# A second landing buffer for float64 weight blocks, and their transfers put forward in the queue, in an attention and mixture-of-experts kernel

## The chip, the cores and the metric

The kernel runs on one core of a Trainium2 chip. The metric is the time of one execution on the device in microseconds (us). Three runs of the kernel before took 558.76, 559.46 and 561.17 us; their median, 559.46 us, is the time to compare with. A separate profiled execution took 557.68 us.

## What is computed

Attention over 8 batches of 8 heads, 576 positions, head size 64, with a block-causal mask of blocks of 64; its output, 4608 rows of 512, goes through a soft mixture of 8 experts, and that through a gated product:

```python
scores = scale * q @ k.T                      # per batch and head, masked, softmax, @ v
logits = x @ phi                              # x: 4608 x 512, phi: 512 x 32
slot_input = softmax(logits, over rows).T @ x
slot_out[e] = relu(slot_input[e] @ w1[e]) @ w2[e]        # 8 experts, 4 slots each
x = softmax(logits, over slots) @ slot_out
a, b = x @ moe2_w1, x @ moe2_w2
out = (a * b) @ moe2_w3 @ moe2_w_out
```

The four matrices named moe2 arrive as float64 (their draws are divided by a float64 number); the kernel narrows them to float32 itself.

## The kernel before

**Attention.** It is tiled by pairs of heads: 32 pairs, numbered n, four to a batch b. For a pair, SP loads queries and keys (`ld`, line 493) and values (`ldv`, 497). ACT and POOL split queries and keys in a high and a low part (506, 513). TensorE makes score tiles for the row maxima (`M`, 526), DVE reduces them (`R`, 530), TensorE turns the maxima (`mT`, 552), ACT copies them out (564), and four small transfers on SP spread them over a row (`mx`, 573 to 575). TensorE then makes the scores (`Q`, 584), ACT the exponentials (`E`, 607), POOL three sums of exponential tiles for the denominators (`P0`, `P1`, `P3`, 617), TensorE the products with the values (`V`, 632 and 636) and the denominators (`SU`, 648, which needs POOL's three sums), and DVE adds these up (664, 666).

**Once per batch, beside the pairs of the next one.** DVE takes reciprocals of the denominators (672), SP writes them to DRAM (`rw`, 677 and 678) and reads them back, each row repeated on 64 partitions (`rd1`, `rd2`, `rd0`, `rd3`, two reads each, 683). POOL multiplies the attention output by them (`sx`, 688, four instructions of which two come ahead of a sum of the pair at hand and two behind it). Then follow the logits (697), transposes (754) and the slots' inputs (803, 805) on TensorE.

**The blocks.** Beside the attention, 28 blocks of 128 rows by 512 float64 numbers (128x1024 in 32-bit words) are narrowed, numbered j: 0 to 7 of w_out, 8, 9, 26 and 27 of w3, 10 to 17 of w1 (into the tile wA), 18 to 25 of w2 (into wB, whose four rows of 1024 fill in order; blocks 24 and 25 write row 3). A block is loaded by one transfer on SP (`bl`, line 1022) into the first 1024 columns of the tile vt; ACT squares the high words (`bm`, 1035), DVE puts the bits together in three instructions (`b1`, `b2`, `b3`: 1028, 1030, 1032) and a fourth writes the narrowed block (`b4`, 1037). All blocks share the one buffer in vt, so the transfer of block j waits for the readers of block j-1.

**What sets the order.** `Plan` holds every step as an operation with an engine, a duration, what it waits for and a due time. `Plan.order` simulates the engines and gives one list, sorted by the simulated start; each engine executes its part of that list strictly in order. SP issues all transfers, so a transfer that waits holds up those behind it. The line that names the waits of a block's transfer is

```python
op("bl", "SP", .43, old(j - 1, "b3", "bm") or [("Q0", 2)], lat=3.5, due="b", ...)
```

**After the attention** (from about 317 us) come the last batch's logits, the product of w3 and w_out (1130), the experts (1151 to 1172, whose weights stream in 2 MB transfers, 1054), and from about 420 us the products 1292, 1355 and 1357 that make the output.

Of the kernel before, what the change touches and what calls it, by code (L numbers as in the profile page):

```python
# [11 lines left out]
I32 = mybir.dt.int32  # L12
# [19 lines left out]
def warm(nc, keep, ps, n, w=128):  # L32

    for _ in range(n):
# [8 lines left out]
           Q0=(36.7116, -4.3567, 26.3714, 15.8153), Q1=(52.1613, 19.992, 71.6173, 44.2372),  # L43
# [39 lines left out]
WAIT = dict(PE=0.0, DVE=10616.85007, ACT=6722.41331, POOL=7334.5673, SP=12439.66901)  # L83
PERIOD, HELD, SLIP, WIN0, WIN1 = 100.0, 8, 0.1, 20, 29
BG0, BGS = 3.0, 1.0
BESIDE = {8: 0, 9: 2, 26: 4, 27: 6}
LATE_W3 = [i for i in range(16) if i not in BESIDE.values()]
PLACE = (0, 4, 1, 5, 2, 6, 3, 7)
# [11 lines left out]
class Plan:  # L100
# [213 lines left out]
    def op(self, key, eng, dur, after=(), banks=0, free=None, mode="full", lat=None, due=None, late=0., load=0., filler=False):  # L314
# [2 lines left out]
                             free=free if free is None or isinstance(free, tuple) else (free, key[1]),  # L317
                             mode=mode if eng == "PE" else None, due=self.due(key[0] if due is None else due) + late)

    def order(self):  # L320
        ops, INF = self.ops, 1e18
        free = dict(PE=4., DVE=2., ACT=2., POOL=3.5, SP=.7)
        bank, held, done, mode, out, queue = [0.] * BANKS, {}, {}, None, [], 0.
        waits, then, ready = {k: len(o["after"]) for k, o in ops.items()}, {}, {e: {} for e in free}
        row = deque(sorted((k for k in ops if ops[k]["eng"] == "PE" and not ops[k]["filler"]), key=lambda k: (ops[k]["due"], ops[k]["at"])))
        fill = deque(k for k in ops if ops[k]["filler"])
        for k, o in ops.items():
            for a in o["after"]:
                then.setdefault(a, []).append(k)
            if not waits[k]:  # L330
                ready[o["eng"]][k] = 0.
        pairs = lambda: [max(bank[i:i + 2]) for i in range(0, BANKS, 2)]
        space = lambda n: min(pairs()) if n == 2 else min(bank) if n else 0.
        while len(out) < len(ops):
            best = None
            for e, R in ready.items():
                can = []
                for k in R if e != "PE" else [k for k in (*list(row)[:1], *list(fill)[:1]) if k in R]:
                    o = ops[k]
                    turn = TURN[mode][o["mode"]] if e == "PE" and mode is not None and o["mode"] != mode else 0.  # L340
                    t = max(R[k], free[e] + turn, space(o["banks"]))
                    if t < INF:
                        can.append((t, k))
                if e == "PE" and len(can) == 2:
                    can = can[1:] if can[1][0] + ops[can[1][1]]["dur"] <= can[0][0] + SLIP else can[:1]
                if can:
                    first = min(t for t, _ in can)
                    c = min((x for x in can if x[0] <= first + LOOK[e]), key=lambda x: (ops[x[1]]["due"] + WAIT[e] * (x[0] - first), ops[x[1]]["at"]))
                    if best is None or c[0] < best[0]:
                        best = c[0], e, c[1]  # L350
            t, e, k = best
            o, slot, idle = ops[k], None, t - free[e]
            del ready[e][k]
            end = t + o["dur"]
            if e == "PE":
                (fill if o["filler"] else row).popleft()
                turn = TURN[mode][o["mode"]] if mode is not None and o["mode"] != mode else None
                if t > free[e] + .01 and not (turn is not None and t <= free[e] + turn + 1e-9):
                    end += ENTRY[o["mode"]]
                mode = o["mode"]  # L360
            if o["banks"] == 2:
                p = pairs()
                i = 2 * p.index(min(p))
                slot = held[k] = (i, i + 1)
            elif o["banks"]:
                can = [i for i in range(BANKS) if bank[i] <= t + 1e-9]
                slot = held[k] = (max(can, key=lambda i: (bank[i ^ 1], -i)) if can else bank.index(min(bank)),)
            for i in slot or ():
                bank[i] = INF
            free[e] = end  # L370
            done[k] = end + o["lat"]
            if e == "SP":
                queue = max(queue, end + 1.3) + o["load"]
                done[k] = max(done[k], queue + .7)
            if o["free"]:
                for i in held[o["free"]]:
                    bank[i] = done[k]
            out.append((t, len(out), k, slot, idle if e == "PE" and k[1] < 2 else 0.))
            for a in then.get(k, ()):
                waits[a] -= 1  # L380
                if not waits[a]:
                    ready[ops[a]["eng"]][a] = max(done[x] for x in ops[a]["after"])
        return [o[2:] for o in sorted(out)]
# [14 lines left out]
class Attn:  # L398
# [577 lines left out]
        self.constants()  # L976

    def run(self):
        for (name, n), slot, idle in Plan(self.nb).order():
            if idle > .5 and (name[0] in "MQ" or name == "mT") and n < 2:  # L980
                warm(self.nc, self.keep, self.bank(slot), int(4.5 * idle - 1), 256)
            f = getattr(self, "op_" + name, None) or getattr(self.rest, "op_" + name, None)
            if f:
                f(n, slot)
            else:
                f = getattr(self, "op_" + name[:-1], None) or getattr(self.rest, "op_" + name[:-1])
                f(n, slot, int(name[-1]) if name[-1].isdigit() else name[-1])


class Rest:  # L990
# [3 lines left out]
    def __init__(self, tc, ctx, io, keep):  # L994
        self.tc, self.nc, self.io, self.keep, self.ctx = tc, tc.nc, io, keep, ctx
        self.pre_ctx = ctx.enter_context(ExitStack())
        self.pre = self.pre_ctx.enter_context(tc.tile_pool(name="pre", bufs=1))
        self.right = ctx.enter_context(tc.tile_pool(name="right", bufs=1, side="right"))
        self.vt = self.pre.tile([128, 1280], F32, name="vt")
        self.wA, self.wB = (self.pre.tile([128, 4, 1024], F32, tag=f"w{m}", name=f"w{m}") for m in "AB")  # L1000
        self.wO = self.pre.tile([128, 8, 512], F32, name="wO")
        self.w01 = self.pre.tile([128, 2, 512], F32, tag="w01", name="w01")
        self.wo_t, self.w3_t = {}, {}
        self.w2 = self.right.tile([128, 512], F32, name="w2")
        self.win, self.u64, self.f64, self.W, self.pairs, self.wos, self.w_terms = {}, {}, {}, {}, {}, {}, {}
        self.st, self.hT, self.stages = {}, {}, {}

    def background(self, j, step, slot):

        nc = self.nc  # L1010
        if j < 8:
            src, dst = self.io["w_out"][128 * j:128 * j + 128], self.wO[:, j]
        elif j in BESIDE:
            i = BESIDE[j]
            src, dst = self.io["w3T"][i // 2, i % 2], self.f(i)
        else:
            w, src = ((self.wA, "moe2_w1"), (self.wB, "moe2_w2"))[(j - 10) // 8]
            row, f = (j - 10) % 8 // 2, 512 * (j % 2)
            src, dst = self.io[src][128 * row:128 * row + 128, 2 * f:2 * f + 1024], w[:, row, f:f + 512]
        if step == "l":  # L1020
            self.raw64 = self.vt[:, 0:1024].bitcast(I32)
            nc.sync.dma_start(out=self.raw64, in_=src)
            return
        v = self.raw64.rearrange("p (n t) -> p n t", t=2)
        lo, hi = v[:, :, 0], v[:, :, 1]
        if step == 1:
            u = self.ub = self.attn.bank(slot).bitcast(I32)
            nc.vector.tensor_scalar(u, hi, 3, 0x3fffffff, op0=ALU.logical_shift_left, op1=ALU.bitwise_and)
        elif step == 2:
            nc.vector.scalar_tensor_tensor(self.ub, hi, -0x40000000, self.ub, op0=ALU.bitwise_and, op1=ALU.bitwise_or)  # L1030
        elif step == 3:
            nc.vector.scalar_tensor_tensor(self.ub, lo, 29, self.ub, op0=ALU.logical_shift_right, op1=ALU.bitwise_or)
        elif step == "m":
            self.m64 = self.vt[:, 1024:1280].bitcast(mybir.dt.bfloat16)
            nc.scalar.activation(out=self.m64, in_=hi.bitcast(F32), func=AF.Square)
        else:
            nc.vector.scalar_tensor_tensor(dst, self.m64, 1.024e-9, self.ub.bitcast(F32), op0=ALU.is_ge, op1=ALU.mult)
# [505 lines left out]
```

## Time and profile before

| what | value |
|---|---|
| median of three runs | 559.46 us |
| profiled execution: whole / span of the instructions | 557.68 / 555.8 us |
| TensorE busy | 543.1 us, 98% |
| DVE, POOL, ACT busy | 394.3, 334.0, 322.6 us |
| granted TensorE clock | 1.000 |
| moved by DMA | 116.97 MB, mean 210 GB/s |

The span is the time from the first instruction to the last; 1.9 us of the execution lie around it. A busy TensorE is not one at its peak, because ends of matmuls are modelled; where it waits is better read from the chain of work that ended last. Of DMA issues the trace shows when SP issued them; when a transfer landed is seen by who waited for it.

### The profile page before, as it was taken

The numbers are of one execution on the slowest core, as the hardware profiler recorded it, in microseconds if no ns is written. First come the engines' busy times: TensorE is split into PE (matmuls) and PEld (weight loads), VectorE is DVE, ScalarE is ACT, GpSimd is POOL, SyncE is SP. The second block draws the span as 40 slices with busy tenths as digits, with TensorE's granted clock in tenths as the row PEclk, the third lists the DMA queues.
The fourth block names the chain that finished last, engine by engine and source line by source line (L and its number), as shares of the span: only waits on it lengthen the run. The fifth ranks groups of instructions, "written<-read, shape, count | busy, mean of one in ns | idle before, by whom it ended". The sixth has DMA issues, their size and how long they took to land.

```text
span 555.8 us, 14186 instructions
## 1 busy us (share of the span) xinstructions
PE 543.1 (98%) x5527; PEld 407.4 (73%) x5527; DVE 394.3 (71%) x721; ACT 322.6 (58%) x636; POOL 334.0 (60%) x244
## 2 busy tenths in 40 slices
PE   8899999999999999999999999899899999999997
PEld 4777878787877787777778675465568678888885
DVE  5778877898898988987975499132849585565550
ACT  3856768677686696686858625123442455444451
POOL 5798997897988988969978526103430122423320
PEclk9999999999999999999999999999999999999999
DMA  7255775556566566476466886999832057557622
GB/s 258 92 161 179 229 277 180 175 178 207 158 204 218 162 210 207 133 223 178 154 197 224 318 354 253 429 424 420 372 101 78 3 159 258 193 181 249 209 103 109
DMA packets 39514, 116.97 MB, mean 210 GB/s; under 512 B 5532, under 2 KB 15996, under 8 KB 37384
## 3 DMA queue, kind: packets, MB, share of 16 engines
q1 hardware_dynamic: 39448, 116.08, 60.8%
q8 instruction: 43, 0.70, 0.5%
q14 instruction: 23, 0.19, 0.1%
HBM read 105.75 MB, written 10.45 MB: 209 GB/s over the span
## 4 chain that ended last, share of the span: by engine, by line
PE 82%; DMA 9%; DVE 4%; ACT 2%; POOL 1%; issue 1%; DVEq 0%; ACTq 0%; POOLq 0%; SPq 0%
PE ps L584 17%; PE ps L1355 16%; PE ps L632 15%; DMA win<-in_moe_w 7%; PE ps L526 6%; PE ps L648 4%; PE ps L1130 4%; PE ps L1292 3%; PE ps L754 3%; PE ps L697 2%; PE ps L1357 1%; PE ps L1172 1%; DVE tc L530 1%; PE ps L803 1%; PE ps L1151 1%
## 5 line engine op out<-in xcount | busy, mean ns | idle before, releaser
L530 DVE TENSOR_REDUCE tc<-ps 128x10 f32<-128x640 f32 (+2 forms) x128 | 122.5, 988 | 27.6 <-PE ps L526 23.9
L607 ACT ACTIVATE s<-ps 128x1024 f32<-128x1024 f32 (+2 forms) x128 | 102.7, 839 | 37.6 <-PE ps L584 30.1
L584 PE MATMUL ps<-set 64*128 64x320 f32 (+4 forms) x1152 | 103.3, 297 | 0.2 <-ACT s L607 0.2
L513 POOL TENSOR_TENSOR set<-raw,set 128x1152 fp32r<-128x1152 f32 x32 | 84.8, 2660 | 7.3 <-ACT set L506 5.7
L584 PEld LDWEIGHTS ps<-set 64*128 64x128 f32 (+1 forms) x1152 | 82.9, 177 | 5.7 <-ACT s L607 0.5
L617 POOL TENSOR_TENSOR tc<-tc,s 128x384 f32<-128x384 f32 (+1 forms) x63 | 80.7, 1281 | 5.4 <-DVE tc L617 0.9
L617 POOL TENSOR_TENSOR tc<-s,s 128x640 f32<-128x640 f32 x32 | 49.9, 1559 | 27.1 <-ACT s L607 15.1
L632 PE MATMUL ps<-s,xw 128*64 128x320 f32 (+3 forms) x528 | 64.0, 384 | 0.0
L1355 PE MATMUL ps<-H,pB 128*128 128x512 f32 x216 | 53.7, 395 | 0.4 <-POOL pB L1335 0.4
L1355 PE MATMUL ps<-H,pA 128*128 128x512 f32 x216 | 52.9, 395 | 0.0
L584 PE MATMUL ps<-shift 64*128 64x320 f32 (+3 forms) x320 | 51.6, 319 | 0.0
L632 PEld LDWEIGHTS ps<-s,xw 128*64 128x64 f32 x528 | 34.4, 137 | 22.4 <-issue 1.2
L526 PE MATMUL ps<-set 64*128 64x320 f32 (+5 forms) x384 | 47.9, 326 | 1.5 <-ACT set L506 1.3
L1368 ACT COPY s<-ps 128x512 f32<-128x512 f32 x35 | 20.5, 585 | 48.5 <-PE ps L1357 48.5
L1355 PEld LDWEIGHTS ps<-H,pB 128*128 128x128 f32 x216 | 40.6, 189 | 10.7 <-POOL pB L1335 1.1
L1355 PEld LDWEIGHTS ps<-H,pA 128*128 128x128 f32 x216 | 40.6, 189 | 9.7 <-DVE pA L1335 0.3
L1335 POOL TENSOR_TENSOR pB<-wx,pB 128x384 fp32r<-128x384 f32 x12 | 16.1, 1343 | 49.3 <-ACT pB L1330 49.3
L1041 POOL TENSOR_TENSOR s<-vt,s 128x512 fp32r<-128x512 f32 x12 | 15.5, 1293 | 38.4 <-ACT s L1043 38.4
L526 PEld LDWEIGHTS ps<-set 64*128 64x128 f32 (+1 forms) x384 | 32.0, 188 | 8.1 <-issue 2.2
L506 ACT CAST set<-raw 128x1152 fp32r<-128x1152 f32 x31 | 35.7, 1154 | 1.1 <-DMA raw<-in_qk 1.1
L584 PEld LDWEIGHTS ps<-shift 64*128 64x128 f32 x320 | 30.6, 187 | 0.7
L1130 PE MATMUL ps<-wx,s 128*128 128x512 f32 x96 | 27.9, 414 | 2.5 <-ACT s L1043 2.3
(283 smaller groups left out, 1033.9 us busy)
## 6 DMA issues: line engine op xcount, KB each, us to landing
win<-in_moe_w SPq DMA_DIRECT2D x13, 2048.0 KB
raw<-in_qk SPq DMA_DIRECT2D x32, 576.0 KB
vt<-in_moe_w SPq DMA_DIRECT2D x16, 512.0 KB
out<-s SPq DMA_DIRECT2D x16, 512.0 KB
shift<-rr SPq DMA_DIRECT2D x56, 144.0 KB
xw<-in_v SPq DMA_DIRECT2D x22, 320.0 KB
xw<-in_moe_w SPq DMA_DIRECT2D x3, 2048.0 KB
s<-in_w3T SPq DMA_DIRECT2D x12, 512.0 KB
```

What stands on the lines that cost most here:

```text
L506: self.nc.scalar.copy(hi, self.raw[n])
L513: self.nc.gpsimd.tensor_tensor(lo, self.raw.pop(n), hi.bitcast(F32), op=ALU.subtract)
L526: self.nc.tensor.matmul(ps[0:m, h, o:o + kn], lhsT=qh[r, q0:q0 + m], rhs=kh[r, k0:k0 + kn], start=True, stop=True)
L530: self.nc.vector.tensor_reduce(self.bmb[n % 2][:, :, o:o + m // 64], self.st.pop(("M", n, i))[:, :, 0:m].rearrange("p h (n k) -> p h n k", ...
L584: mm = lambda h, o, n, lt, rt, m=128, **k: self.nc.tensor.matmul(ps[0:m, h, o:o + n], lhsT=lt, rhs=rt, **k)
L607: self.nc.scalar.activation(out=out, in_=ps[:, :, 0:sum(g[3] for g in self.UNITS[u])], func=AF.Exp, scale=SCALE)
L617: eng.tensor_tensor(acc[:, :, lo:hi], a, b, op=ALU.add)
L632: mm(ps[64 * h:64 * h + 64, q0 - lo:q1 - lo], lhsT=v[:, 128 * j + 64 * h:128 * j + 64 * h + 64], rhs=pt[:, h, o:o + q1 - q0], start=j == 0 ...
L648: mm = lambda g, o, rhs, **k: self.nc.tensor.matmul(ps[32 * g:32 * g + 32, o:o + rhs.shape[-1]], lhsT=one, rhs=rhs, **k)
L1130: self.nc.tensor.matmul(self.st["W", f], lhsT=a[:, o], rhs=b, start=j == 0, stop=j == 23)
L1355: nc.tensor.matmul(ps, lhsT=a[:, k, r], rhs=b[:, k], start=k + i == 0, stop=False)
L1368: nc.scalar.copy(o[:, h], bank(u, t))
```

## The change

Blocks with an odd number below 24 land in row 3 of wB, which is not written before block 24; all others land in vt as before. After `Plan.order` has made its list, the new function `ahead` moves the transfers of blocks 1 to 24 forward in it: each to a place whose simulated start is 3.5 us (`LEAD`) ahead of the block's own, not ahead of the last readers of block j-2 (`b3`, `bm`), and not where a maxima transfer (`mx`) would start within 2.5 us after it. Waits between instructions follow the buffers that they use, so up to block 24 a transfer now waits for the readers of the block two before it. The simulated starts, and so the order of all other operations, stay as they were.

```diff
+LEAD = 3.5
+    def ahead(self):
+        out = self.order()
+        where = lambda k: next(i for i, x in enumerate(out) if x[0] == k)
+        for j in range(1, 25):
+            i = where(("bl", j))
+            lo = 1 + max(where(k) for k in ([("b3", j - 2), ("bm", j - 2)] if j > 1 else [("Q0", 2)]))
+            t = self.began["bl", j]
+            maxima = [self.began[x[0]] for x in out[lo:i] if x[0][0] == "mx"]
+            far = lambda u: all(not u <= m < u + 2.5 for m in maxima)
+            k = next((q for q in range(i, lo - 1, -1) if self.began[out[q][0]] <= t - LEAD and far(self.began[out[q][0]])), None)
+            if k is None:
+                k = next((q for q in range(lo, i) if far(self.began[out[q][0]])), i)
+            out.insert(k, out.pop(i))
+        return out
     def order(self):
-        ops, INF = self.ops, 1e18
+        ops, INF, self.began = self.ops, 1e18, {}
...
+            self.began[k] = t
             out.append((t, len(out), k, slot, idle if e == "PE" and k[1] < 2 else 0.))
...
-        for (name, n), slot, idle in Plan(self.nb).order():
+        for (name, n), slot, idle in Plan(self.nb).ahead():
...
         if step == "l":
-            self.raw64 = self.vt[:, 0:1024].bitcast(I32)
-            nc.sync.dma_start(out=self.raw64, in_=src)
+            self.raw64[j] = (self.wB[:, 3] if j % 2 and j < 24 else self.vt[:, 0:1024]).bitcast(I32)
+            nc.sync.dma_start(out=self.raw64[j], in_=src)
             return
-        v = self.raw64.rearrange("p (n t) -> p n t", t=2)
+        v = self.raw64[j].rearrange("p (n t) -> p n t", t=2)
```

On TensorE, DVE, ACT and POOL the order of the instructions is the same in both kernels; only SP's queue differs (line 1022 before is 1039 now; lines after the new function are 15 to 17 higher).

SP's queue where batch 2's reciprocals (rr0) are read back, before; vt_88 is the blocks' buffer, and the block is number 10:

```order
L574 DMA shift_117<-wx_103 2x64
L575 DMA shift_117<-wx_103 2x64
L683 DMA shift_117<-rr0_62 64x576 x4
L493 DMA raw0_106<-in_qk 128x1152
L683 DMA shift_117<-rr0_62 64x576 x4
L1022 DMA vt_88<-in_moe2_w1 128x1024
L497 DMA xw_104<-in_v 128x640
```

and now:

```order
L591 DMA shift_117<-wx_103 2x64
L592 DMA shift_117<-wx_103 2x64
L700 DMA shift_117<-rr0_62 64x576 x4
L1039 DMA vt_88<-in_moe2_w1 128x1024
L510 DMA raw0_106<-in_qk 128x1152
L700 DMA shift_117<-rr0_62 64x576 x4
L514 DMA xw_104<-in_v 128x640
```

The block has gone ahead of the load of a pair's queries and keys and of the last four of the eight reads. Blocks 6, 14, 18 and 22 move in the same way in batches 1, 3, 4 and 5, and block 3 passes four of batch 0's reads.

SP's queue where batch 5's reciprocals (rr1) are written, before; the block is number 21:

```order
L575 DMA shift_117<-wx_103 2x64
L493 DMA raw1_107<-in_qk 128x1152
L677 DMA rr1_63<-tc_100 4x256
L678 DMA rr1_63<-tc_100 4x320
L677 DMA rr1_63<-tc_100 4x256
L678 DMA rr1_63<-tc_100 4x320
L1022 DMA vt_88<-in_moe2_w2 128x1024
```

and now, with the second buffer wB_90:

```order
L592 DMA shift_117<-wx_103 2x64
L1039 DMA wB_90<-in_moe2_w2 128x1024
L510 DMA raw1_107<-in_qk 128x1152
L694 DMA rr1_63<-tc_100 4x256
L695 DMA rr1_63<-tc_100 4x320
L694 DMA rr1_63<-tc_100 4x256
L695 DMA rr1_63<-tc_100 4x320
```

The block has gone ahead of the load of queries and keys and of the four writes; blocks 5, 9, 13 and 17 move in the same way. The other moved blocks pass loads of values, of which some are followed by maxima transfers.

## Rows read from the trace of the kernel before

**Rows 1.** The page: busy time of TensorE, and engines of the chain.
```profile
PE 543.1 (98%) x5527; PEld 407.4 (73%) x5527; DVE 394.3 (71%) x721; ACT 322.6 (58%) x636; POOL 334.0 (60%) x244
...
PE 82%; DMA 9%; DVE 4%; ACT 2%; POOL 1%; issue 1%; DVEq 0%; ACTq 0%; POOLq 0%; SPq 0%
```

**Rows 2.** The chain in time (start us, us, what): logits of batches, one DVE piece.
```profile
143.15 1.24 DVE tc L530
...
153.82 1.46 PE ps L697 x64
...
191.79 1.46 PE ps L697 x64
...
229.77 1.46 PE ps L697 x64
```

**Rows 3.** The chain from 225 to 262 us: block 21 and what follows.
```profile
242.54 5.02 DMA vt<-in_moe_w
...
248.23 1.01 ACT s L607
...
249.28 0.86 PE ps L648 x11
```

**Rows 4.** Waits of ACT, 30 to 310 us (total us, times, longest).
```profile
ACT vt L1035 <- DMA vt<-in_moe_w: 1.8, 4, 0.7
```

**Rows 5.** Timeline of ACT, 245 to 250 us (start, us; idle before in brackets).
```profile
247.64 0.68 ACT L1035 ACTIVATE vt<-vt 128x512 bf16<-128x512 f32 x1 [0.34 <-DMA vt<-in_moe_w]
```

**Rows 6.** Waits of SP's queue over the whole span, at the blocks' transfer.
```profile
SPq L1022 <- DVE ps L1032: 3.3, 5, 0.8
...
SPq L1022 <- DMA win<-in_moe_w: 1.2, 1, 1.2
```

**Rows 7.** Timeline of SP: writes, reads and blocks of batches 2, 3, 5.
```profile
128.95 0.29 SPq L678 DMA_DIRECT2D rr<-tc  x1
...
132.82 3.11 SPq L683 DMA_DIRECT2D shift<-rr  x4
...
136.60 2.54 SPq L683 DMA_DIRECT2D shift<-rr  x4
139.27 0.50 SPq L1022 DMA_DIRECT2D vt<-in_moe_w  x1
...
175.58 2.36 SPq L683 DMA_DIRECT2D shift<-rr  x4
...
249.76 2.37 SPq L683 DMA_DIRECT2D shift<-rr  x4
```

**Rows 8.** Stretches: length, busy PE, PEld, DVE, ACT, POOL, clock, DMA share, GB/s.
```profile
136.00:146.00 10.00, 9.93 (x131) 7.76 (x130) 8.28 (x15) 5.33 (x10) 9.52 (x7) 1.00 0.87 243
...
345.00:360.00 15.00, 13.14 (x131) 5.60 (x129) 4.24 (x7) 3.78 (x10) 2.57 (x2) 1.00 1.01 428
```

**Rows 9.** Timeline of POOL: multiplications and the sums behind them, batches 2, 3, 5.
```profile
143.32 2.79 POOL L688 TENSOR_TENSOR xw<-xw,shift 128x576 f32<-128x576 f32 x2 [0.30 <-DMA shift<-rr]
...
147.71 2.66 POOL L617 TENSOR_TENSOR tc<-tc,s 128x640 f32<-128x640 f32 x2
...
181.04 2.81 POOL L688 TENSOR_TENSOR wx<-wx,shift 128x576 f32<-128x576 f32 x2
...
185.44 2.65 POOL L617 TENSOR_TENSOR tc<-tc,s 128x640 f32<-128x640 f32 x2
...
257.10 2.79 POOL L688 TENSOR_TENSOR wx<-wx,shift 128x576 f32<-128x576 f32 x2
...
261.50 2.66 POOL L617 TENSOR_TENSOR tc<-tc,s 128x640 f32<-128x640 f32 x2
```

**Rows 10.** Timeline of TensorE: first denominator matmul behind those sums.
```profile
151.18 0.40 PE L648 MATMUL ps<-s,tc 128*32 128x256 f32 x1
...
189.15 0.40 PE L648 MATMUL ps<-s,tc 128*32 128x256 f32 x1
...
264.34 0.40 PE L648 MATMUL ps<-s,tc 128*32 128x256 f32 x1
```

More of the change, by code (lines that the diff above doesn't have):

```diff
@@ L1002, in __init__ @@
         self.w01 = self.pre.tile([128, 2, 512], F32, tag="w01", name="w01")
-        self.wo_t, self.w3_t = {}, {}
+        self.wo_t, self.w3_t, self.raw64 = {}, {}, {}
         self.w2 = self.right.tile([128, 512], F32, name="w2")
```

## The prediction

> **What bounds the kernel now.** I read the page first: TensorE is busy 98% of the span, and 82% of the chain that ended last is its own work [rows 1]. That alone doesn't say that it never waits, since the ends of matmuls are modelled, so the next view is the chain in order of time. From 30 to 240 us it lies on TensorE but for one DVE piece of 1.24 us in each batch (six in all, one shown). The logits of three successive batches start 37.97 and 37.98 us apart [rows 2]. What differs from batch to batch, such as when a block's transfer lands, leaves no mark on that period.
>
> The change is about transfers, so I looked where a block's transfer is on the chain. There is one such place: the transfer of block 21, issued at 242.54 us, is followed for 5.02 us, then come ACT's exponentials at 248.23 and the denominators on TensorE at 249.28 [rows 3]. The waits of ACT say how much there is altogether: between 30 and 310 us ACT waited four times for a block, 1.8 us in total, at most 0.7 at once [rows 4]. At block 21 it was 0.34 us [rows 5].
>
> **The change, part by part.**
>
> *The second buffer.* It takes away a wait of SP, not of an engine that computes: SP waited five times for the last reader in vt, 3.3 us in total, at most 0.8 [rows 6]. DVE's and ACT's instructions read from another address, their number and sizes are the same, and their order too. I cost this part at nothing: SP's waits are hidden behind TensorE's period, which is the same in batches with and without them. If that cover were gone, it would be worth a part of the 3.3 us.
>
> *The transfers put forward: what is gained.* They should be there before ACT wants them. Of the 1.8 us, the 0.34 us at block 21 lies on the chain. The other three waits lie in stretches where the chain is on TensorE, in batches whose period is 37.97 us like the others. So I take 0.34 us; the ends are 0 (TensorE, busy with slots' inputs until then, may start the denominators no sooner) and 1.8 us.
>
> By the Trainium skill ("Trainium Kernel Development and Optimization", Best Practices) one double-buffers for performance, to overlap transfers with computing; by that rule the whole 1.8 us would come back. The trace agrees only at block 21; elsewhere the one buffer overlaps well enough.
>
> *What is moved back: the reads of the reciprocals.* Blocks 6, 10, 14, 18 and 22 are now issued before a load of queries and keys and before the last four reads of a batch's reciprocals. In batch 2 these reads were issued from 136.60 us on, the block after them at 139.27 [rows 7], and POOL waited for the reads: its third multiplication started at 143.32 us after 0.30 us idle [rows 9]. The four multiplications themselves have time, as logits follow 9 us later, at 153.82 [rows 2]. But POOL works in order: behind the last two stand the three sums of the next pair, and the denominators on TensorE wait for these.
>
> What a block costs the reads behind it, the trace of before doesn't show directly. It is 128x1024 words of 4 bytes, 0.524 MB. At 428 GB/s, the rate of the stretch where the queue never runs dry, that is 1.22 us; at the 243 GB/s of the stretch in question it is 2.16 us. And it could be nothing, if the block's packets fall into holes: in that stretch the engines stood idle for 13% of 10 us, 1.3 us [rows 8]. I take 1.22 us: the DMA share of the stretch is 0.87, nearer to the full queue, and the rate of 243 has the small broadcast reads in it.
>
> The Trainium skill ("DMA: Bandwidth & Descriptors", Queues, rings and completion order) says that on each DMA engine descriptors are consumed in ring order, and that SP owns one row of rings. By that rule whatever SP issues behind a block waits for its bytes, so early blocks are not free; by a rule of free overtaking this term would be nothing.
>
> How much of 1.22 us reaches TensorE is read from where the sums end and the denominators start:
> - Batch 5: sums end at 261.50 + 2.66 = 264.16 [rows 9], the denominators start at 264.34 [rows 10]. The 0.18 us between them is the least that I see, so here TensorE was already waiting for POOL and there is no room. But the reads came in time: from their issue to the multiplication it took 257.10 - 249.76 = 7.34 us, against 143.32 - 136.60 = 6.72 us in batch 2, where they were late. I count the difference, 0.62 us, as room in the reads. Cost 1.22 - 0.62 = 0.60 us.
> - Batch 2: sums end at 150.37, denominators at 151.18; 0.81 less the 0.18 is 0.63 us of room, none in the reads. Cost 0.59 us.
> - Batch 3: sums end at 188.09, denominators at 189.15; 1.06 less 0.18 is 0.88 us. The reads took only 181.04 - 175.58 = 5.46 us until they were used, so I assume that they were just in time. Cost 0.34 us.
> - Batches 0, 1 and 4: POOL doesn't wait for reads and I take nothing.
>
> Together 0.60 + 0.59 + 0.34 = 1.53 us. A delay of TensorE is kept to the end, as its chain goes on without a gap; the DVE piece in each batch answers to a matmul of TensorE's own and moves with it. At 2.16 us the three would cost 1.54 + 1.53 + 1.28 = 4.35 us; with blocks in holes nothing.
>
> *What else is passed.* Five blocks go ahead of the writes of the reciprocals. In batch 2 the last write was issued at 128.95 us and the first read at 132.82 [rows 7], so a write that lands later by part of a block's 1.22 us may still be in time; I take nothing, and at worst the reads are later by 1.22 us more, which the upper end holds for one batch. The other blocks pass loads of values, which SP issues after a wait for the buffer of an earlier pair, so the block fills a pause of SP. Cost nothing; a maxima transfer that is late would hold up TensorE's scores directly, which is in the upper end as well.
>
> *The sum.* 1.53 - 0.34 = +1.2 us: the profiled execution would go from 557.68 (span 555.8 and 1.9 around it) to 558.9 us. The median of the runs stands 1.8 us above the profiled one, at 559.46, so I forecast 560.7 us for the median.
>
> **The rivals.**
>
> *Only the gain.* The blocks fall into holes of the queue, no read is late, and all of ACT's 1.8 us count: 557.7 us. For it speaks the 13% of idle time, against it that POOL already waits for reads in batch 2, and that periods don't differ.
>
> *Slower, by late reads.* Same place as my term, but with a block at 2.16 us: 4.35 us and no gain, 563.8 us. It decides from the point where three blocks cost 2.8 us after the gain: 3p - 2.13 - 0.34 = 2.8, so p = 1.76 us a block. For it speaks the rate of the stretch itself, against it that this rate is that of small reads.
>
> *The transfers don't come earlier in fact.* SP issues in order, and its waits stand in the queue too: once a block waited 1.2 us for the landing of a 2 MB load [rows 6]. A block that is put behind such a wait would be issued when it was before. Then nothing changes: 559.5 us. Against it: around the reads in batch 2 SP issues without a pause.
>
> *Faster by more.* If DVE's earlier work on blocks shortened the DVE piece in all six batches by half, it would give 6 x 0.62 = 3.7 us: 555.8 us. Against it: the chain enters this piece from a matmul, so DVE was not late there.
>
> **How the numbers follow.** My forecast, a little slower, has a chance of 0.47; only the gain 0.17; no earlier in fact 0.13; slower by late reads 0.16; faster by more 0.07. About 0.5%, 2.8 us, is what a measurement of this kernel can tell from no change. The first three lie inside it: same 0.77, faster 0.07, slower 0.16. The range has my forecast, the unchanged case and the gain with the three runs' scatter, and most of the way to the slower case, below its full price: 557.6 to 563.2 us.
>
> **What would show it.** Right: no wait of ACT for a block any more, the denominators near 249 us up to 0.34 us earlier against the logits before them; POOL's waits for the reads grow in batches 2 and 3 and appear in batch 5, and the periods of these batches grow by some tenths. Wrong: periods unchanged at 37.97 us although blocks are issued earlier (the price of a block is hidden), POOL without waits for reads (no ring order), a longer period also in batches 1 and 4 (price over 1.8 us), or TensorE waiting for a maxima transfer.

## The result, and the profile after

The changed kernel takes 567.91 us (median of four runs, 565.58 to 572.78) where the kernel before took 559.75 us beside it: a ratio of 1.0144, 95% interval 1.0103 to 1.0184. It is slower by about 8 us. The forecast was 560.7 us with a range up to 563.2, so the forecast was wrong. The profiled execution took 565.58 us, its span is 563.8 us against 555.8. Medians and ratios, here and below, leave out executions more than 1.5% longer than the fastest of the same kernel: three of the ten of one experiment, and two of the kernel before (566.29 and 1689.54 us).

The page of the changed kernel (busy time; engines of the chain that ended last), beside [rows 1]:

```profile
PE 545.1 (97%) x5527; PEld 408.9 (73%) x5527; DVE 395.0 (70%) x721; ACT 322.4 (57%) x636; POOL 333.8 (59%) x244
...
PE 73%; DMA 12%; DVE 6%; POOL 4%; issue 2%; ACT 1%; SPq 1%; POOLq 0%; DVEq 0%; ACTq 0%
```

The busy times are nearly those of before. The chain is not: TensorE's share fell from 82 to 73%, and DMA, DVE and POOL rose from 9, 4 and 1% to 12, 6 and 4%. No engine has more instructions; some waits have come onto the path. The same chain in order of time tells where, by the starts of the logits, as in [rows 2]:

```profile
80.00 1.46 PE ps L714 x64
...
118.00 1.46 PE ps L714 x64
...
157.46 1.46 PE ps L714 x64
...
195.79 1.46 PE ps L714 x64
...
235.59 1.46 PE ps L714 x64
...
275.25 1.46 PE ps L714 x64
```

From one start to the next it is now (us; "reads first" is an experiment below):

| up to the logits of batch | before | changed | reads first |
|---|---|---|---|
| 1 | 37.93 | 38.00 | 37.94 |
| 2 | 37.97 | 39.46 | 37.98 |
| 3 | 37.97 | 38.33 | 37.97 |
| 4 | 37.98 | 39.80 | 38.00 |
| 5 | 37.10 | 39.66 | 36.85 |
| 6 | 26.25 | 26.25 | 26.25 |

Four of the six periods are clearly longer; all six are 6.30 us longer together. Another 2.08 us is there at the first logits already (80.00 against 77.92 us); it arises before the first moved transfer and is treated at the end of this section. What comes after the attention is 0.4 us shorter.

What a longer period is made of, read from the chain of the changed kernel at batch 4 (start us, us, what):

```profile
215.66 0.54 SPq L1039
...
216.33 0.33 SPq L510
216.71 0.46 SPq L700
217.21 8.53 DMA shift<-rr
...
227.24 1.43 POOL xw L705
...
231.90 1.00 POOL tc L634
232.95 0.85 PE ps L665 x9
```

SP issues block 18 (L1039), then the load (L510), then the last four reads of the reciprocals (L700). From the issue of the second of these the chain waits 8.53 us for reads, goes through POOL's multiplications and the three sums, and ends at the denominators on TensorE. Before, the chain stayed on TensorE here but for DVE's 1.24 us. POOL's waits between 30 and 310 us (total us, times, longest), where the kernel before had one of 0.30 us [rows 9]:

```profile
POOL xw L705 <- DMA shift<-rr: 6.6, 3, 2.9
POOL wx L705 <- DMA shift<-rr: 5.0, 3, 3.0
```

and TensorE's in the same stretch, the longest kind of its waits:

```profile
PE ps L665 <- POOL tc L634: 4.0, 3, 2.0
```

Six waits, one in each of batches 0 to 5; three times TensorE itself stops for them. The multiplications that were late in batches 2 and 5, from POOL's timeline (compare [rows 9]):

```profile
147.77 2.80 POOL L705 TENSOR_TENSOR xw<-xw,shift 128x576 f32<-128x576 f32 x2 [2.55 <-DMA shift<-rr]
...
265.68 2.81 POOL L705 TENSOR_TENSOR wx<-wx,shift 128x576 f32<-128x576 f32 x2 [2.97 <-DMA shift<-rr]
```

and the denominators of batch 5 on TensorE's timeline (compare [rows 10], where they started at 264.34 us; matmuls of one line that follow each other are drawn together):

```profile
270.15 0.62 PE L665 MATMUL ps<-s,tc 128*32 128x256 f32 x2
272.75 0.46 PE L665 MATMUL ps<-tc 128*32 128x320 f32 x1 [1.98 <-POOL tc L634]
...
272.77 0.61 PE L665 MATMUL ps<-s,tc 128*32 128x128 f32 x3
```

SP's queue in batch 2, beside [rows 7]: the last four reads are issued 4.06 us after the first (139.12 - 135.06), before it was 3.78. Issue is thus only 0.3 us of the 2.2 us by which these reads land later (table below).

```profile
135.06 2.91 SPq L700 DMA_DIRECT2D shift<-rr  x4
...
139.12 3.11 SPq L700 DMA_DIRECT2D shift<-rr  x4
```

What the change was to give, it gives: the instruction of ACT that reads a block waits for no transfer any more (the list of waits has no line for L1052 where [rows 4] had 1.8 us), and block 21 is there when ACT comes to it, with no idle time in brackets where [rows 5] had 0.34 us:

```profile
253.00 0.68 ACT L1052 ACTIVATE vt<-wB 128x512 bf16<-128x512 f32 x1
```

That this is worth time isn't seen in this trace; the experiments come back to it.

*The 2.08 us at the start.* The rows by stretch of the changed kernel (length, busy PE, PEld, DVE, ACT, POOL, granted clock, DMA share, GB/s):

```profile
10.00:15.60 5.60, 3.17 (x28) 1.84 (x27) 5.24 (x14) 2.28 (x5) 1.96 (x2) 1.00 0.69 237
15.60:22.40 6.80, 6.80 (x53) 5.72 (x53) 3.56 (x7) 4.11 (x7) 3.80 (x2) 0.50 0.54 176
```

After a stretch in which TensorE was busy only 3.17 of 5.60 us, its granted clock stood at 0.50, the lower of its levels (1.2 of 2.4 GHz), for 6.8 us. The instructions up to there are the same in both kernels, and the first moved transfer is issued only at 39.03 us. The two executions part earlier still: twelve matmuls that start at 5.23 us took 1.16 us together, in the profiled execution of before 1.92 us. The delay is whole at the end of the stretch: by the trace the second pair's scores start at 23.40 us where they started at 21.41, and it stays at 2.0 us until batch 0 is done. The experiment that only adds the second buffer has such a stretch too, takes the time of before, and starts its first logits at 80.64 us:

```profile
16.40:23.30 6.90, 6.90 (x55) 5.90 (x54) 3.77 (x7) 3.58 (x7) 4.08 (x2) 0.51 0.54 170
```

Among all runs of the kernel before the mean granted clock went from 0.982 to 1.000 and the time with it: ten runs at 1.000 took 558.1 us in the mean, nineteen at 0.994 took 559.6, ten at 0.988 took 562.9 and two at 0.982 took 565.2. The profiled execution of before happened to have 1.000. So these 2 us belong to the execution, not to the change, and the change's own part is the 6.3 us of the periods. Runs at the same mean clock bear this out: at 0.994 the changed kernel took 565.58 and 567.22 us, 6.0 and 7.6 us more than the kernel before, and at 0.982 572.78 us, 7.6 us more. Whether the change also lowers the clock, four runs don't tell.

### The profile page after: what moved, and what is told of

It is laid out like the page before. It is cut to its first block, busy times and chain, and to the rows that moved or that the text cites. A ratio compares the mean times of both kernels' runs of the same rounds, so it can differ in the third digit from the quotient of the medians.

```text
span 563.8 us, 14189 instructions
## 1 busy us (share of the span) xinstructions
PE 545.1 (97%) x5527; PEld 408.9 (73%) x5527; DVE 395.0 (70%) x721; ACT 322.4 (57%) x636; POOL 333.8 (59%) x244
## 4 chain that ended last, share of the span: by engine, by line
PE 73%; DMA 12%; DVE 6%; POOL 4%; issue 2%; ACT 1%; SPq 1%; POOLq 0%; DVEq 0%; ACTq 0%
PE ps L1372 16%; PE ps L601 15%; PE ps L649 13%; DMA win<-in_moe_w 7%; PE ps L1147 4%; PE ps L543 4%; PE ps L665 4%; PE ps L1309 3%; DMA shift<-rr 3%; PE ps L771 3%; DVE tc L547 2%; POOL tc L634 2%; PE ps L714 2%; DMA raw<-in_qk 2%; PE ps L1374 1%
## 5 line engine op out<-in xcount | busy, mean ns | idle before, releaser
L601 PE MATMUL ps<-set 64*128 64x320 f32 (+4 forms) x1152 | 105.0, 300 | 0.2 <-ACT s L624 0.2
L601 PEld LDWEIGHTS ps<-set 64*128 64x128 f32 (+1 forms) x1152 | 84.7, 180 | 5.7 <-ACT s L624 0.5
L543 PEld LDWEIGHTS ps<-set 64*128 64x128 f32 (+1 forms) x384 | 31.8, 184 | 8.8 <-ACT set L523 3.0
L665 PE MATMUL ps<-s,tc 128*32 128x64 f32 (+2 forms) x384 | 29.8, 294 | 0.4
```

Source lines behind the costliest of these rows:

```text
L543: self.nc.tensor.matmul(ps[0:m, h, o:o + kn], lhsT=qh[r, q0:q0 + m], rhs=kh[r, k0:k0 + kn], start=True, stop=True)
L601: mm = lambda h, o, n, lt, rt, m=128, **k: self.nc.tensor.matmul(ps[0:m, h, o:o + n], lhsT=lt, rhs=rt, **k)
L665: mm = lambda g, o, rhs, **k: self.nc.tensor.matmul(ps[32 * g:32 * g + 32, o:o + rhs.shape[-1]], lhsT=one, rhs=rhs, **k)
```

## The experiments

Each was timed beside the kernel before on the same chip. Lines are numbered as in the changed kernel; in "load behind" and "both behind" they are 3 higher, and in "before, load behind" 8 higher than in the kernel before.

| kernel | median us | before us | ratio (95% interval) |
|---|---|---|---|
| second buffer only | 560.70 | 560.66 | 0.9990 (0.9957 to 1.0024) |
| reads first | 560.33 | 560.66 | 0.9995 (0.9971 to 1.0020) |
| only past the reads | 564.05 | 560.66 | 1.0079 (1.0035 to 1.0124) |
| writes first | 565.70 | 560.66 | 1.0108 (1.0068 to 1.0148) |
| half width | 562.97 | 561.68 | 1.0029 (0.9992 to 1.0065) |
| half rows | 562.56 | 561.68 | 1.0028 (0.9991 to 1.0066) |
| load behind | 560.27 | 561.68 | 0.9980 (0.9951 to 1.0008) |
| both behind | 560.20 | 561.68 | 0.9959 (0.9932 to 0.9987) |
| both behind, again | 560.07 | 560.67 | 1.0003 (0.9972 to 1.0035) |
| before, load behind | 562.11 | 560.67 | 1.0030 (1.0002 to 1.0059) |

From each trace I also worked out when the third pair of reads (the one that POOL's third multiplication needs) had landed, counted from the issue of a batch's first read. When a transfer landed is taken from its completions in the trace. Batches 2 to 5, and how long POOL stood idle ahead of that multiplication. One execution of each kernel was traced; those of only past the reads (573.25 us) and half width (567.96 us) were the longest of their ten:

| kernel | landed after (us) | mean | POOL idle (us) |
|---|---|---|---|
| before | 10.37, 9.07, 9.13, 9.70 | 9.57 | 0.30, 0.03, 0, 0 |
| second buffer only | 10.79, 9.73, 10.13, 9.18 | 9.96 | 0.66, 0, 0, 0 |
| changed | 12.58, 10.90, 12.56, 12.35 | 12.10 | 2.55, 1.35, 2.89, 2.97 |
| reads first | 10.29, 9.74, 9.13, 9.25 | 9.60 | 0.24, 0, 0, 0 |
| writes first | 12.57, 11.77, 11.22, 12.28 | 11.96 | 2.41, 1.83, 1.08, 2.21 |
| only past the reads | 12.91, 13.45, 13.19, 12.74 | 13.07 | 2.77, 3.29, 3.03, 2.66 |
| half width | 11.64, 11.83, 11.22, 10.60 | 11.32 | 1.74, 2.82, 1.52, 1.21 |
| half rows | 12.44, 10.81, 10.41, 10.43 | 11.02 | 2.39, 1.14, 0.97, 1.04 |
| load behind | 9.01, 9.17, 10.80, 10.51 | 9.87 | 0, 0, 1.02, 0.88 |
| both behind | 6.95, 6.45, 6.34, 6.59 | 6.58 | 0, 0, 0, 0 |
| both behind, again | 6.64, 6.37, 6.41, 6.47 | 6.47 | 0, 0, 0, 0 |
| before, load behind | 7.05, 6.37, 6.74, 6.63 | 6.70 | 0, 0, 0, 0 |

In before, second buffer only and reads first the same transfers stand among these reads, and their means differ by up to 0.4 us; so much comes from the execution alone.

**Is it the buffer or the order?** Second buffer only:

```diff
-        for (name, n), slot, idle in Plan(self.nb).ahead():
+        for (name, n), slot, idle in Plan(self.nb).order():
```

> Only the second buffer; every transfer stands in SP's queue where it stood before. Theory 1 (the loss is reads of reciprocals that land late because blocks were put ahead of them): as before, 559.7 us, within 0.3%, the logits of batches 37.1 to 38.0 us apart, POOL waiting for the reads no longer than the 0.30 us of before. Rival (the second buffer itself, read by DVE and ACT at another address, or a start at half clock that belongs to the program): 562 us or more, or a granted clock under 1.000.

It takes the time of before. The buffer costs and gives nothing that can be measured; the loss is in the order of SP's queue. (POOL waited 0.66 us for reads in batch 2, more than the 0.30 that was expected.) Its trace shows two things more. In batch 3 ACT waited 1.17 us for a block that wasn't put forward, and that period is 38.52 us, 0.55 longer than before: a late block can reach the path. And the period to batch 5 is 36.83 us where it was 37.10, though block 21 stands where it stood before:

```profile
233.00 1.46 PE ps L714 x64
...
269.83 1.46 PE ps L714 x64
```

**Which of the moved blocks?** Reads first (the six blocks that passed the reads stay behind them; the other 18 move):

```diff
-        for j in range(1, 25):
+        for j in [1, 2, 4, 5, 7, 8, 9, 11, 12, 13, 15, 16, 17, 19, 20, 21, 23, 24]:
```

> The change, but blocks 3, 6, 10, 14, 18 and 22 stay behind the reads of the reciprocals, where they were before; the other 18 are put forward. Theory 1 (late reads): most of the 8 us goes, 559.5 to 561 us, POOL's third multiplication waits no more than 0.5 us in any batch. Rival, late writes (blocks 5, 9, 13, 17 and 21 ahead of the writes): 564 to 568 us, POOL still waits 1 us and more for the reads, since they need the writes. Rival, clock: as the change, 566 to 568 us, with a granted clock under 0.995.

The whole loss is gone, and the periods are those of before (table above). From its chain:

```profile
229.00 1.46 PE ps L714 x64
...
265.85 1.46 PE ps L714 x64
```

and of its POOL's waits for the reads one is left:

```profile
POOL xw L705 <- DMA shift<-rr: 0.2, 1, 0.2
```

The period to batch 5 is 36.85 us where it was 37.10. This looks like the gain at block 21, but it isn't shown to be: second buffer only has 36.83 us and before, load behind 36.87 us, where block 21 is issued behind the writes as before and ACT doesn't wait for it. The 0.34 us of [rows 5] is a wait of that one execution.

Only past the reads (the six blocks alone):

```diff
-        for j in range(1, 25):
+        for j in [3, 6, 10, 14, 18, 22]:
```

> Only blocks 3, 6, 10, 14, 18 and 22 are put forward, past the reads; the other 18 stay where they were before. Theory 1 (late reads): 564 to 567 us, most of the loss of the change; POOL's third multiplication idle for 1 to 3 us in batches 2 to 5. Rival, late writes: 560 to 561 us. With the price of 1.22 us a block that was predicted: 560.7 us.

The six blocks alone bring more than half of the loss back, 0.8% (4.4 us) where the change has 1.4%, with the reads late in each of batches 2 to 5.

Writes first (the five blocks that passed the writes stay behind them; the other 19 move):

```diff
-        for j in range(1, 25):
+        for j in [1, 2, 3, 4, 6, 7, 8, 10, 11, 12, 14, 15, 16, 18, 19, 20, 22, 23, 24]:
```

> The change, but blocks 5, 9, 13, 17 and 21 stay behind the writes of the reciprocals, where they were before; the other 19 are put forward. Theory 1 (late reads): 565 to 568 us, as the change or 1 to 2 us less. Rival, late writes: 560 to 562 us.

It keeps most of the loss, 5 us at the median, 1.1%. Late writes are not the main cause. They aren't free either: the table above counts from the issue of the first read and doesn't show when that is. In batch 5 the first read is issued at

```profile
246.67 2.40 SPq L683 DMA_DIRECT2D shift<-rr  x4
...
253.19 2.39 SPq L700 DMA_DIRECT2D shift<-rr  x4
```

before and in the changed kernel. POOL was free for its third multiplication 10.43 us after it before (257.10, [rows 9]) and 9.52 us in the changed kernel (265.68 less the idle 2.97); in batch 4 it was 10.21 and 9.81 us. All seven traces with blocks 17 and 21 ahead of the writes have 9.47 to 9.90 us in these two batches, the other five, writes first among them, 10.16 to 10.43. So with these blocks ahead the reads start later against POOL's work, in the changed kernel by 0.4 and 0.9 us. SP's timeline shows where: in the seven SP pauses for 0.42 to 0.86 us between the maxima transfers ahead of the reads, in the five for 0.05 us. Reads first is one of the seven and loses nothing, as its reads still land 0.74 and 0.35 us before POOL multiplies; behind a block there is no such margin, so up to 1.3 us of the change's loss may come from here (an estimate, 0.4 + 0.9).

This run shows a second price. TensorE waits 2.00 us for the sums in batch 5, and then its clock falls (TensorE's timeline; the third row is the same three matmuls that took 0.61 us above):

```profile
267.51 0.62 PE L665 MATMUL ps<-s,tc 128*32 128x256 f32 x2
270.13 0.74 PE L665 MATMUL ps<-tc 128*32 128x320 f32 x1 [2.00 <-POOL tc L634]
...
270.15 1.05 PE L665 MATMUL ps<-s,tc 128*32 128x128 f32 x3
```

The stretches (granted clock is the third number from the end):

```profile
266.00:270.00 4.00, 2.13 (x26) 1.49 (x22) 2.02 (x6) 2.05 (x2) 3.84 (x3) 0.99 0.30 82
270.00:273.40 3.40, 3.27 (x30) 2.70 (x32) 0.69 (x3) 0.53 (x1) 3.40 (x3) 0.51 0.00 0
273.40:280.00 6.60, 6.60 (x128) 5.02 (x125) 5.99 (x15) 4.84 (x14) 5.80 (x4) 1.00 0.63 213
```

3.4 us at half clock cost about 1.7 us (an estimate: half of it) beside the 2.00 us of the wait. In the changed kernel's trace the wait of 1.98 us at the same place was not followed by it, so this happens in some executions only. Nor does it belong to late reads: near 390 us TensorE waits 2.30 us for ACT both in the kernel before and in reads first, and half clock for 3.4 us followed in reads first but not in the kernel before.

**What is the price made of?** Half width (six blocks loaded with half the bytes in as many packets) and half rows (with half the packets); both leave out the other half of these six blocks:

```diff
-            nc.sync.dma_start(out=self.raw64[j], in_=src)
+            q = slice(0, 512 if j in (3, 6, 10, 14, 18, 22) else 1024)
+            nc.sync.dma_start(out=self.raw64[j][:, q], in_=src[:, q])
```

> The change, but blocks 3, 6, 10, 14, 18 and 22 are only half loaded: the first 512 of their 1024 words a row, so as many packets of half the size (the other half of these six blocks is left out). Theory, the price of a block is its bytes: half of the 2 to 4 us by which the reads land later, the third multiplication idle under 1 us in batches 1 and 3 and 1 to 1.7 us in 2, 4 and 5; 561 to 563 us. Rival, the price is per packet or per transfer (place in the queue, issue): 566 to 568 us as the change.

```diff
-            nc.sync.dma_start(out=self.raw64[j], in_=src)
+            q = slice(0, 64 if j in (3, 6, 10, 14, 18, 22) else 128)
+            nc.sync.dma_start(out=self.raw64[j][q], in_=src[q])
```

> The change, but of blocks 3, 6, 10, 14, 18 and 22 only 64 of the 128 rows are loaded: half the packets, of full size (the other half of these six blocks is left out). Theory, bytes: 561 to 563 us, as with half the width. Theory, per packet: 561 to 563 us here too, while half the width stays at 566 or more. Rival, per transfer (issue and place in the queue alone): 566 to 568 us.

Both come out at 562.6 to 563.0 us, 0.3% above before, with intervals that reach just below 1. Their waits of POOL, half width first:

```profile
POOL wx L705 <- DMA shift<-rr: 4.3, 3, 2.8
POOL xw L705 <- DMA shift<-rr: 4.0, 4, 1.7
```

```profile
POOL wx L705 <- DMA shift<-rr: 2.9, 3, 1.1
POOL xw L705 <- DMA shift<-rr: 1.0, 1, 1.0
```

A whole block puts the reads back by 12.10 - 9.57 = 2.53 us, half of one by 1.75 or 1.45. The number of packets does not decide, and the place in the queue alone does not either, as half the bytes cost less with the same place. So the price seems to go mostly with the bytes, but that isn't shown cleanly: half a block costs more than half, the batches scatter by 1 us and the means by 0.4.

**Is a block worse than other bytes?** Load behind (the changed kernel, with the load of queries and keys put behind the last four reads in batches 0 to 5):

```diff
+        for b in range(6):
+            i = next(q for q in range(where(("rd2", b)), len(out)) if out[q][0][0] == "ld")
+            out.insert(max(where(("rd0", b)), where(("rd3", b))), out.pop(i))
         return out
```

> The change, with one thing more: in batches 0 to 5 the load of queries and keys that stood between the block and the last four reads goes behind these reads, so that about as many bytes are ahead of them as before (0.52 MB of block instead of 0.59 MB of load). Theory, all bytes ahead of the reads count alike: 559 to 561 us, the third multiplication idle 0.5 us at most; the load has 3 us and more until ACT wants it. Rival, it is the block itself that disturbs the reads (its packets, or the buffer it writes): 564 to 567 us.

With the block ahead of the reads but the load behind them the time is that of before, and what is left of POOL's waits (0.5 us at most was expected) is

```profile
POOL xw L708 <- DMA shift<-rr: 1.0, 1, 1.0
POOL wx L708 <- DMA shift<-rr: 0.9, 1, 0.9
```

A block is no worse than a load. Taking the load from behind to ahead of the reads (both behind, then reads first) puts them back by 9.60 - 6.58 = 3.02 us for 0.590 MB, 5.1 us for each MB; a block by 2.53 us for 0.524 MB, 4.8 us for each MB.

**Is there something to gain?** Both behind (reads first and load behind together: nothing big between the eight reads), run twice:

> Blocks 3, 6, 10, 14, 18 and 22 behind the reads as before, the other 18 put forward, and the load of queries and keys behind the reads as well: nothing big between the eight reads of a batch. If reads were still late somewhere on the path (0.24 to 0.30 us of idle POOL in batch 2, batch 5): 558.5 to 559.5 us where the kernel before has 559.7, so 0 to 0.2% faster. Rival, the load is then late for ACT: 561 us or more.

> The kernel of both_behind once more, in five rounds beside the former. If its 0.4% is real: 0.2 to 0.6% faster than before with an interval below 1; where the clock is 1.000 the gain should be only the 0.25 us at block 21 and the 0.3 us of POOL. Rival, scatter: within 0.2% of before.

Its edit is that of reads first and that of load behind together. The first time (ten runs) it was 0.4% faster, the second time (twelve) there was no difference, so the 0.4% is not borne out. SP's queue in it, in batch 5:

```profile
246.68 4.96 SPq L703 DMA_DIRECT2D shift<-rr  x8
251.74 0.54 SPq L513 DMA_DIRECT2D raw<-in_qk  x1
```

Its profiled execution had a granted clock of 1.000, as that of before, so these two can be laid side by side: 556.90 against 557.68 us. The 0.8 us is a seventh of one per cent and below what a comparison can tell. POOL never waits for the reads here: with these 3 us earlier than before next to nothing is left to gain from them.

Before, load behind (the kernel before, with the three lines of load behind applied to the list of `order` and nothing else):

> The kernel before, one buffer and no block put forward, with one edit: in batches 0 to 5 the load of queries and keys goes behind the last four reads of the reciprocals. If the 0.4% that both_behind gained comes from the reads: the same here, 0.2 to 0.5% faster than before, reads landing 6 to 7 us after the first is issued instead of 9 to 10, POOL never waiting for them. Rival, it came from the blocks put forward: the same time as before within 0.2%. Rival, it was scatter of the granted clock: no difference here and in the repetition.

It is no faster, against the expectation, but 0.3% slower; its interval leaves out 1 only just, as that of the 0.4% above did. The reads never make POOL wait, but two other transfers came late. SP's timeline in batch 0 shows the load put behind the last two reads, and ACT's timeline the wait for it, ahead of the first logits; in batch 1 ACT waits for a block, and the chain goes over that block's transfer:

```profile
65.63 0.53 SPq L501 DMA_DIRECT2D raw<-in_qk  x1
```

```profile
72.17 1.15 ACT L514 CAST set<-raw 128x1152 fp32r<-128x1152 f32 x1 [2.42 <-DMA raw<-in_qk]
...
109.97 0.69 ACT L1043 ACTIVATE vt<-vt 128x512 bf16<-128x512 f32 x1 [1.58 <-DMA vt<-in_w_out]
```

```profile
102.48 7.41 DMA vt<-in_w_out
```

The first logits start 1.27 us later than before, of which the start of the program has a part, and the second 38.53 us after them, not 37.93. The load is late because it was put behind the reads; whether the block's delay comes from that too isn't shown.

None of the runs points to a version that is measurably faster than the kernel before.

## Why the prediction was wrong

*What bounds the kernel, and the second buffer:* right. TensorE's period bounds it, and the buffer alone changes nothing (0.9990).

*The gain at block 21:* the wait is gone, as was said, but no gain is shown. A period 0.25 us shorter is there also where block 21 wasn't put forward, with the second buffer only and without it; the 0.34 us was read from one execution. The near match in size is luck. ACT's other waits gave nothing in the compared trace, as was said; late by 1.17 and 1.58 us in two experiments, a block cost 0.55 and 0.60 us. The Trainium skill's rule that one double-buffers for performance ("Trainium Kernel Development and Optimization", Best Practices) is not borne out here: 1.8 us of waits went away, and of that at most 0.25 us came back.

*Where the loss would come from:* right. The prediction named the last reads, POOL's third multiplication, the sums and the denominators, and this is the chain of the changed kernel. The Trainium skill's rule that a DMA engine consumes descriptors in ring order ("DMA: Bandwidth & Descriptors", Queues, rings and completion order) fits: behind a block the reads landed after 12.10 us, not 9.57.

*The price of a block, "I take 1.22 us":* this step failed. It measured 2.53 us in the mean of batches 2 to 5, twice what was taken and above the upper end of 2.16. The rate of 428 GB/s was taken from a stretch with other transfers. The view of DMA packets of the kernel before, for 345 to 360 us and for 178 to 182 us, where the last reads of batch 3 land:

```profile
DMA packets 440, 6.42 MB, mean 428 GB/s; under 512 B 48, under 2 KB 48, under 8 KB 48
...
DMA packets 453, 1.09 MB, mean 272 GB/s; under 512 B 80, under 2 KB 80, under 8 KB 453
...
q1 hardware_dynamic: 453, 1.09, 101.5%
```

At 428 GB/s most packets are of 8 KB and more, 14.6 KB in the mean (nearly all bytes come from the 2 MB transfers); among the reads all are smaller, 2.4 KB in the mean, and with the engines fully busy (101.5%) they move 272 GB/s. A high DMA share was read as the rate of the fastest stretch, and it doesn't give that. At 272 GB/s a block is 1.93 us. Two stretches of the changed kernel, in which the last reads of batch 4 land (the last two numbers are DMA share and GB/s):

```profile
218.00:222.00 4.00, 4.00 (x56) 3.28 (x54) 3.02 (x5) 1.67 (x4) 4.00 (x4) 1.00 0.92 281
222.00:226.00 4.00, 3.93 (x58) 3.24 (x58) 3.34 (x7) 3.07 (x5) 1.11 (x2) 1.00 0.87 199
```

By these a block is 1.87 or 2.63 us, on both sides of the 2.53. The 243 GB/s of the stretch itself was thus the nearer of the two ends, and the 428 the wrong choice; why one stretch moves 199 and another 281 at nearly the same share, these runs don't show.

*The room:* right in sum, less so in parts. Of POOL's delay 2.55 us in batch 2 (0.30 was there before), 1.35 in batch 3 (0.03) and 2.97 in batch 5, the periods grew by 1.49, 0.36 and 2.56 us, so the rooms behind the reads were 0.76, 0.96 and 0.41, where the prediction had 0.63, 0.88 and 0. That TensorE was already waiting in batch 5 was misread: its list of waits between 30 and 310 us before is empty. With the prices measured in the three batches, 2.21, 1.83 and 2.65 us, the prediction's rooms (0.63, 0.88, 0.62) would have given 1.58, 0.95 and 2.03 us, 4.56 us in sum; the three periods sum to 4.41 us. So the path was right, and the price is what the sum failed on. The rival "slower, by late reads" had 4.35 for the same three, with a block at 2.16.

*"Batches 0, 1 and 4: POOL doesn't wait for reads and I take nothing":* right for 0 and 1 (no growth and 0.07 us), wrong for 4. That POOL doesn't wait says only that the reads are early, not by how much: by the completions they had 1.08 us in batch 4 and 2.14 us in batch 1. The reads came 3.43 us later in batch 4 and 2.56 us in batch 1; that goes through the first margin, and what is left over from the second was nearly hidden. Batch 4 cost 1.82 us. At 1.22 us a block next to nothing would have got through the 1.08, so this term failed with the price.

*The writes and the loads of values, cost nothing:* right where the reads aren't also passed (reads first has no loss). Together with a block ahead of the reads the blocks ahead of the writes may cost up to 1.3 us, as said at writes first; the two weren't separated.

*Sum:* forecast 1.53 - 0.34 = +1.2 us; found 4.41 + 1.82 + 0.07 = +6.3 us. Between the two profiled executions the last 2 us of the 8 are the half clock at the start. Between the medians they are not that: the 1.8 us that the prediction added to the profiled execution of before already stand for the lower clock of its other runs, of which 70 of 81 have less than 1.000. The four runs of the changed kernel had 0.982 to 0.994, and at the same clock the difference was 6.0 to 7.6 us; what the 8 us hold beyond that goes with the clock. Part of that may be the change's own, as a wait of 2 us can be followed by a stretch at half clock; how much, these runs don't settle.

*Of the signs named beforehand,* two came true that were to mean "wrong": a longer period in batch 4, and by that a price over 1.8 us a block. POOL's waits for the reads grew where the signs of "right" had them, in batches 2, 3 and 5, but these periods grew by up to 2.56 us instead of some tenths. TensorE waited for a maxima transfer once, 0.2 us, as it did once (0.6 us) in reads first, which lost nothing.

## What to carry to other kernels

A transfer that is put forward in a shared, in-order queue is paid for by whatever it passes, so list these and look up who waits for each; here at most 0.25 us was gained at the blocks and 6.3 us lost at small reads. Price the passed bytes at the rate of that very stretch, with its packet sizes, not at the best rate that the queue reaches elsewhere. Where an engine shows no wait for a transfer, find how early the transfer lands before calling a delay free: the waits list only what is already late. And look at a wait of some tenths in a second execution before counting on its removal.

## What the runs showed of the hardware that I had not expected

- The DMA engines can be busy all the time at 272 GB/s (packets of 2.4 KB in the mean) or 428 GB/s (14.6 KB): the share alone doesn't give the rate.
- Waits of TensorE of 2.00 us (writes first) and 1.61 us (only past the reads, at 196.61 us) were followed by about 3.4 us at half clock, so a late transfer can cost nearly twice what it delays; waits of 1.98 us (changed) and 2.30 us (before) weren't. The length of the wait alone doesn't decide.
- The mean granted clock of the very same kernel went from 0.982 to 1.000 between executions, and its time with it (mean 558.1 us at 1.000, 562.9 at 0.988). Executions should be compared at the same clock.
